# P in two pieces, pinned loads for the second mixture, and another hand-written opening

## The chip, the cores and the metric

The kernel runs on one core of one Trainium2 chip. The metric is the device time of one execution in microseconds, here the median of three runs of the kernel before: 829.34 us (828.67 to 830.78).

## The reference, cut to what matters

Four batches of an attention with eight heads go through two mixtures (two-layer networks). A short P (32 rows per head) first attends to K and V; its result is then both the keys and the values for Q.

```python
q, k, v: (4, 8, 576, 64)     p: (4, 8, 32, 64)
p_packed = sm_attn(p, k, v)              # softmax(p k^T / 8) v, 32 rows per head
out = sm_attn(q, p_packed, p_packed)     # 576 rows per head
x = out as (2304, 512)                   # tokens by (head, dim)
h = x @ w1_in;  x = (h * tanh(softplus(h))) @ w1_out     # 512 -> 2048 -> 512, Mish
h = x @ w2_in;  y = elu(h) @ w2_out                      # 512 -> 2048 -> 512, ELU
```

All four weights arrive as float64; the kernel reads them as pairs of 32-bit words and makes float32 numbers out of them itself.

## The kernel before, in words

**Weights.** A weight tile is 128 rows by 512 float64 numbers (512 KB). `load_raw` (L123) issues its load on SP's queue. `decode` (L135) gives the steps s0 to s5 that turn it into float32: s0 on ACT rescales one word in place (for the first eight tiles with the function Prelu, L158, otherwise with Copy, L160); s1 to s3 on DVE shift and join the words (L165, L173, L178); for w1o and w2 tiles s4 on ACT makes the upper part (L200) and s5 on DVE the rest (L206), since each product is made of three matmuls on upper and lower parts. Tiles of w1i go without s4 and s5: they are folded first (`fold`, L511: the product of the packed P with w1i, L519, which gives the weights G of this batch for the first layer; its two DVE subtractions and ACT copies are in `post`). Half of the tiles of the second mixture are decoded while the first mixture runs, split, and written back to HBM ("staged", L192). Their raw tiles have a pool of two buffers of their own (`sg`).

**Attention.** `scores1` multiplies K by P (L302), after DVE has turned both by 32x32 blocks (kT at L281, pT at L781). Its maximum is taken on DVE (L316), its exponentials on ACT (L321). `transpose_a1` turns the result on PE (L348), `packed` multiplies by V (L373) and turns the packed P (L403 to L406, PT). `scores2` multiplies Q by PT (`pe_rows`, L426), turns the scores on DVE (L455), and makes softmax on DVE and ACT (L462 to L471); `back` turns the result into the layer's input x as an upper and a lower part, a2h and a2l.

**Mixture 1** runs over 128 steps of one block of 288 tokens and 128 of the 2048 columns: `gemm1` (L550 to L552), `mish` on ACT and DVE (L559 to L561), and `gemm2` (L578 to L580) two steps later. The 32 tiles of w1 are decoded as they are needed; attention of the next batch and folds are put in between. In steps 34 to 93 `step_w2` decodes staged tiles of the second mixture. **Mixture 2** (L633 to L678) does the same with blocks of 512 tokens.

**What sets the order.** The first batch's attention, the decoding of the first eight tiles of w1 (indices 0 to 7: four of w1i, four of w1o) and the fold of the first 512 columns are written by hand: the list `order` in `startup` (L785) is the order on PE, DVE, ACT and SP there. `hk` and `hq` are the turns of K and Q, `sc`, `ta`, `pk` the steps of `scores1`, `transpose_a1` and `packed` for the two halves of the heads, `s2` those of `scores2`, `f0` those of the fold, `parts(n, i, ...)` the steps s_i of tile n. All other code is ordered by the compiler's scheduler, which may move an instruction ahead of those written before it when its inputs and its buffer are free; `keep_in_program_order` ties an instruction behind the one traced last on its engine. Each engine and each queue works strictly in order. In the opening, K, Q and weights are issued on SP's queue, V on ACT's, P on both (L756); a load also waits until the load eight places earlier has landed, because eight completion semaphores go round.

Of the kernel before, what the change touches and what calls it, by code (L numbers as in the profile page):

```python
# [9 lines left out]
F32 = mybir.dt.float32  # L10
F32R = mybir.dt.float32r
I32 = mybir.dt.int32
# [25 lines left out]
WSCALE = 2.0 ** 8  # L38
# [3 lines left out]
def kernel(  # L42
# [12 lines left out]
    nc = tc.nc  # L55
    B, H, S, D = q.shape
    NP = p.shape[2]
# [15 lines left out]
    dp = ctx.enter_context(tc.tile_pool(name="dp", bufs=3))  # L73
# [8 lines left out]
    def slot(shape, dt, name):  # L82
        return up.tile(shape, dt, tag="u", name=name)
# [27 lines left out]
        return spare.pop()[:, 1, :]  # L111

    ident = const.tile([128, 128], F32, name="ident")
    pT = const.tile([128, B * H // 2, 2, NP], F32, name="pT")

    y_dr = [dr.tile([128, 4, HALF], F32, name=f"y_dr{i}") for i in range(2 * B)]
    w2_dr = {}
# [5 lines left out]
    def load_raw(name, r, c):  # L123
        nm = f"raw_{name}{r}_{c}"
        t = slot([128, 1024], I32, nm) if name[1] == "1" else sg.tile([128, 1024], I32, tag="sg", name=nm)
        nc.sync.dma_start(
            out=t, in_=weights[name][r * 128:(r + 1) * 128, c * 1024:(c + 1) * 1024]
        )
        raws[name, r, c] = t

    w1v = {}
# [3 lines left out]
    def decode(name, r, c, staged=False, exps=False):  # L135
        raw = raws.pop((name, r, c))
        rr = raw.rearrange("p (n two) -> p n two", two=2)
        w0, w1 = rr[:, :, 0], rr[:, :, 1]
        t = dp.tile([128, 512], I32, tag="dec", name="dec")
        f1 = w1.bitcast(F32)  # L140
        whole = name == "w1i"
        key = {"w1i": (c, r // 2), "w2i": (name, c, r // 2)}.get(name, (name, r // 2))
        if staged:
            if r % 2 == 0:
                w2_dr[key] = dr.tile([128, 2, 2, 512], F32, name=f"w2_dr{name}{r}_{c}")
            parts = raw.bitcast(F32R).rearrange("p (x n) -> p x n", x=2)
        elif r % 2 == 0:
            if whole:
                w1v[key] = slot([128, 2, 512], F32, f"w1v{c}_{r}")
            else:  # L150
                wt[key] = [(small if name == "w2o" and r >= 12 else slot)([128, 2, 512], F32R, f"{name}{x}{r}_{c}") for x in "hl"]
        oi = w1v[key][:, r % 2, :].bitcast(I32) if whole else t

        def s0():
            tc.keep_in_program_order(
                nc.scalar.activation(out=f1, in_=f1, func=ACTF.Prelu, scale=REBIAS, alpha=2.0 ** 32)  # L158
                if exps
                else nc.scalar.activation(out=f1, in_=f1, func=ACTF.Copy, scale=REBIAS)  # L160
            )

        def s1():
            tc.keep_in_program_order(
                nc.vector.tensor_scalar(  # L165
                    out=t, in0=w1, scalar1=3, scalar2=0xFFFFFFF8 - 2 ** 32 if exps else 0x7FFFFFF8,
                    op0=ALU.logical_shift_left, op1=ALU.bitwise_and,
                )
            )

        def s2():
            if not exps:
                nc.vector.scalar_tensor_tensor(  # L173
                    out=t, in0=w1, scalar=-0x80000000, in1=t, op0=ALU.bitwise_and, op1=ALU.bitwise_or
                )

        def s3():
            nc.vector.scalar_tensor_tensor(  # L178
                out=oi, in0=w0, scalar=29, in1=t, op0=ALU.logical_shift_right, op1=ALU.bitwise_or
            )  # L180

        def s4():
            if whole:
                if r % 2 == 1:
                    nc.gpsimd.dma_start(out=w1_dr[c * 2 + r // 2], in_=w1v[key])
            else:
                split_hi(t.bitcast(F32), parts[:, 0] if staged else wt[key][0][:, r % 2, :], 1.0 / WSCALE)

        def s5():
            if staged:  # L190
                split_lo(t.bitcast(F32), parts[:, 0], parts[:, 1], 1.0 / WSCALE)
                nc.gpsimd.dma_start(out=w2_dr[key][:, r % 2], in_=parts.bitcast(F32))  # L192
            elif not whole:
                hi, lo = wt[key]
                split_lo(t.bitcast(F32), hi[:, r % 2, :], lo[:, r % 2, :], 1.0 / WSCALE)

        return [s0, s1, s2, s3, s4, s5]

    def split_hi(val, hi, factor=1.0):
        nc.scalar.activation(out=hi, in_=val, func=ACTF.Copy, scale=factor)  # L200
# [90 lines left out]
    def scores1(b, s):  # L291
        d = {}

        def pe():
            ps = pm()
            d["pair"] = last_pair[0]
            for x in range(2):
                for g in (3, 2, 1, 0):
                    kg = kT[b, g].rearrange("p e s -> p (e s)").rearrange("p (j x t) -> p j x t", x=2, t=32)
                    for th in range(2):  # L300
                        r = 64 * s + 32 * th
                        nc.tensor.matmul(  # L302
                            out=ps[th][32 * g:32 * g + 32, 0:HALF],
                            lhsT=pT[r:r + 32, b * 4 + g, x, :],
                            rhs=kg[r:r + 32, :, x, :],
                            start=(x == 0),
                            stop=(x == 1),
                        )
            if s:
                for g in range(4):  # L310
                    kT.pop((b, g))
# [199 lines left out]
    def fold(b, c):  # L511
# [17 lines left out]
            for s in range(2):  # L529
                split(d["ps"][s], G[b, c][0][:, s, :], G[b, c][1][:, s, :], 1.0 / WSCALE)  # L530

        return [pe, post]


    gt1, ht = {}, {}
# [212 lines left out]
    DEC1 = P["DEC1"]  # L748

    def startup():  # L750
        pr = slot([128, B * H // 2, D], F32, "pr")
        ps_ = p.rearrange("b (g s) n d -> s n (b g) d", s=2)
        for s in range(2):
            for th in range(2):
                r = 64 * s + 32 * th
                (nc.sync, nc.scalar)[s].dma_start(out=pr[r:r + 32], in_=ps_[s])  # L756
        make_identity(nc, ident)
        if WARM:
            wu = ps_h.tile([128, 512], F32, tag="h", name="warm")
# [18 lines left out]
        def parts(n, *which):  # L778
            return [dec[n][i] for i in which]

        nc.vector.transpose(  # L781
            out=pT.rearrange("p g x k -> p (g x k)"), in_=pr.rearrange("p g d -> p (g d)")
        )
        a1t0, a1t1 = ta
        order = [  # L785
            hk[0][0], hk[1][0], hk[2][0], hk[3][0], sc[0][0], sc[1][0], *parts(0, 0), *parts(0, 1, 3, 4, 5),
            sc[0][1], *parts(1, 0), sc[1][1], *parts(1, 1, 3, 4, 5), sc[0][2], a1t0[0], a1t0[1], pk[0][0], a1t1[0], a1t1[1],
            hq[0][0], hq[1][0], sc[1][2], *parts(2, 0), *parts(3, 0), pk[0][1], pk[1][0], hq[2][0], hq[3][0], pk[1][1], pk[0][2],
            *parts(2, 1, 3), pk[1][2], s2[0], *parts(2, 4, 5), *parts(3, 1, 3, 4, 5), f0[0], s2[1], s2[2],
            s2[3], s2[4], *parts(4, 0), f0[1], s2[5], *parts(4, 1, 3), s2[6], *parts(4, 4), s2[7], *parts(4, 5),  # L790
            *parts(5, 0, 1, 3, 4, 5), *parts(6, 0, 1, 3, 4, 5), *parts(7, 0, 1, 3, 4, 5),
        ]
        for o in order:
            o()
# [153 lines left out]
```

## Time and profile before

| | us |
|---|---|
| median of three runs | 829.34 |
| lowest, highest | 828.67, 830.78 |
| the profiled execution's own time | 830.86 |
| its span in the trace | 829.1 |
| PE busy in the span | 777.5 (94%) |
| DVE busy | 440.1 (53%) |
| ACT busy | 346.6 (42%) |

The span lies 1.76 us below the time of the execution that it belongs to. Busy shares over the whole span hide the stages: what counts is read from stretches of it. "Idle before" in a row is the time in which the engine stood still ahead of it, and behind the arrow stands what ended that. PEclk is the clock granted to TensorE as a share of 2.4 GHz.

### The profile page before, as it was taken

How to read it: one execution, taken by the hardware profiler on the slowest of the kernel's cores; microseconds unless marked ns; L12 is line 12 of the kernel's file. 1: busy time of each engine (PE TensorE's matmuls, PEld its weight loads, DVE VectorE, ACT ScalarE, POOL GpSimd, SP SyncE). 2: the span in 40 equal slices, each digit the busy share in tenths (PEclk: the TensorE clock that was granted, in tenths of full speed). 3: DMA queues.
4: the chain of work that ended last, by engine and by line, in shares of the span. 5: the costliest groups of instructions: out<-in, count | busy, mean ns of one | idle time of the engine just before them, and what ended most of it. 6: DMA issues, size and time to landing. Idle time of an engine off the chain costs nothing.

```text
span 829.1 us, 13056 instructions
## 1 busy us (share of the span) xinstructions
PE 777.5 (94%) x5212; PEld 671.0 (81%) x5212; DVE 440.1 (53%) x844; ACT 346.6 (42%) x676; POOL 22.6 (3%) x46
## 2 busy tenths in 40 slices
PE   3656898999999999999999999999999999999997
PEld 3344788979989898899998888888888888888886
DVE  3678788675587466772516753513253334342342
ACT  1265774557465655674534432312141223221222
POOL 0000000000101000000000000000000000000000
PEclk7565998999999999999999999999999999999999
DMA  9954377237656656431592310200020001000000
GB/s 273 372 215 158 120 272 220 81 111 222 197 198 244 191 142 233 142 116 51 180 332 79 127 52 26 76 1 1 1 76 14 1 0 51 13 0 1 26 26 26
DMA packets 69181, 96.80 MB, mean 117 GB/s; under 512 B 36096, under 2 KB 44800, under 8 KB 69120
## 3 DMA queue, kind: packets, MB, share of 16 engines
q1 hardware_dynamic: 62176, 77.22, 29.6%
q0 software_dynamic: 4736, 17.30, 5.3%
q10 hardware_dynamic: 2208, 1.44, 0.7%
q8 instruction: 41, 0.67, 0.3%
q14 instruction: 20, 0.16, 0.1%
HBM read 73.92 MB, written 22.02 MB: 116 GB/s over the span
## 4 chain that ended last, share of the span: by engine, by line
PE 85%; DVE 6%; ACT 4%; DMA 3%; issue 1%; SPq 0%; ACTq 0%; DVEq 0%
PE h L640 8%; PE h L641 8%; PE h L642 8%; PE o L663 8%; PE o L664 8%; PE o L665 8%; PE acc L579 7%; PE acc L578 7%; PE acc L580 7%; PE h L550 4%; PE h L551 4%; PE h L552 4%; PE pm L519 1%; DMA raw_w1i<-in_moe_w_in_dram 1%; DMA raw_w2i<-in_moe_w_in_dram 1%
## 5 line engine op out<-in xcount | busy, mean ns | idle before, releaser
L578 PE MATMUL acc<-gh,w1oh 128*128 128x288 f32 x512 | 150.1, 300 | 5.6 <-ACT w1oh L200 3.4
L579 PE MATMUL acc<-gl,w1oh 128*128 128x288 f32 x512 | 152.8, 300 | 0.1
L580 PE MATMUL acc<-gh,w1ol 128*128 128x288 f32 x512 | 152.3, 300 | 0.0
L641 PE MATMUL h<-yl,w2ih 128*128 128x512 f32 (+1 forms) x320 | 117.7, 368 | 0.0
L642 PE MATMUL h<-yh,w2il 128*128 128x512 f32 (+1 forms) x320 | 117.5, 368 | 0.0
L640 PE MATMUL h<-yh,w2ih 128*128 128x512 f32 (+1 forms) x320 | 116.7, 368 | 0.0
L663 PE MATMUL o<-w2oh,gh 128*128 128x512 f32 x288 | 112.4, 390 | 1.1 <-ACT ob L269 0.7
L664 PE MATMUL o<-w2ol,gh 128*128 128x512 f32 x288 | 112.2, 390 | 0.0
L644 ACT ACTIVATE t<-h 128x512 f32<-128x512 f32 (+1 forms) x80 | 42.8, 553 | 165.3 <-PE h L642 157.5
L665 PE MATMUL o<-w2oh,gl 128*128 128x512 f32 x288 | 108.3, 389 | 0.0
L645 DVE TENSOR_SCALAR t<-t 128x512 f32<-128x512 f32 (+1 forms) x80 | 31.7, 399 | 142.3 <-ACT t L644 141.5
L578 PEld LDWEIGHTS acc<-gh,w1oh 128*128 128x128 f32 x512 | 96.9, 192 | 10.1 <-ACT w1oh L200 3.8
L579 PEld LDWEIGHTS acc<-gl,w1oh 128*128 128x128 f32 x512 | 97.7, 191 | 6.5 <-DVE gl L561 3.2
L580 PEld LDWEIGHTS acc<-gh,w1ol 128*128 128x128 f32 x512 | 97.5, 191 | 5.0 <-issue 4.5
L561 DVE TENSOR_TENSOR gl<-t,gh 128x288 fp32r<-128x288 f32 x128 | 57.8, 453 | 77.9 <-ACT gh L560 77.3
L550 PE MATMUL h<-a2h,gh 128*128 128x288 f32 x256 | 78.7, 310 | 14.4 <-ACT a2h L200 10.5
L559 ACT ACTIVATE t<-h 128x288 f32<-128x288 f32 x128 | 52.2, 409 | 81.4 <-PE h L552 80.1
L551 PE MATMUL h<-a2l,gh 128*128 128x288 f32 x256 | 77.8, 304 | 2.9 <-DVE a2l L204 2.9
L200 ACT ACTIVATE gh<-t 128x512 fp32r<-128x512 f32 (+1 forms) x80 | 46.6, 588 | 78.6 <-DVE t L646 49.5
L552 PE MATMUL h<-a2h,gl 128*128 128x288 f32 x256 | 77.1, 303 | 0.0
L204 DVE TENSOR_TENSOR gl<-t,gh 128x512 fp32r<-128x512 f32 (+1 forms) x80 | 50.3, 638 | 41.0 <-ACT gh L200 39.5
L642 PEld LDWEIGHTS h<-yh,w2il 128*128 128x128 f32 x320 | 60.3, 188 | 10.3
(107 smaller groups left out, 1101.5 us busy)
## 6 DMA issues: line engine op xcount, KB each, us to landing
w1r<-w_dr SPq DMA_DIRECT2D x24, 512.0 KB, 6.4
raw_w2i<-in_moe_w_in_dram SPq DMA_DIRECT2D x16, 512.0 KB, 4.4
raw_w1i<-in_moe_w_in_dram SPq DMA_DIRECT2D x16, 512.0 KB, 8.1
raw_w1o<-in_moe_w_out_dram SPq DMA_DIRECT2D x16, 512.0 KB, 8.1
raw_w2o<-in_moe_w_out_dram SPq DMA_DIRECT2D x16, 512.0 KB, 3.7
k<-in_k_dram SPq DMA_DIRECT2D x16, 288.0 KB, 4.6
y_dr<-y POOLq DMA_DIRECT2D x16, 288.0 KB, 2.9
w_dr<-w1v POOLq DMA_DIRECT2D x8, 512.0 KB, 5.1
```

The lines of the kernel that those rows point to most:

```text
L550: nc.tensor.matmul(out=hp, lhsT=wh, rhs=xh, start=(kt == 0), stop=False)
L551: nc.tensor.matmul(out=hp, lhsT=wh, rhs=xl, start=False, stop=False)
L552: nc.tensor.matmul(out=hp, lhsT=wl, rhs=xh, start=False, stop=(kt == 1))
L578: nc.tensor.matmul(out=o, lhsT=wh[:, cs], rhs=gh, start=first, stop=False)
L579: nc.tensor.matmul(out=o, lhsT=wh[:, cs], rhs=gl, start=False, stop=False)
L580: nc.tensor.matmul(out=o, lhsT=wl[:, cs], rhs=gh, start=False, stop=last)
L640: nc.tensor.matmul(out=hp, lhsT=wh, rhs=xh, start=(i == 0), stop=False)
L641: nc.tensor.matmul(out=hp, lhsT=wh, rhs=xl, start=False, stop=False)
L642: nc.tensor.matmul(out=hp, lhsT=wl, rhs=xh, start=False, stop=(i == 3))
L663: nc.tensor.matmul(out=o, lhsT=gh[:, ts], rhs=wh, start=(kk == 0), stop=False)
L664: nc.tensor.matmul(out=o, lhsT=gh[:, ts], rhs=wl, start=False, stop=False)
L665: nc.tensor.matmul(out=o, lhsT=gl[:, ts], rhs=wh, start=False, stop=(kk == NK - 1))
```

## The change

P is loaded as two tiles, one for batch 0 (a quarter of it, on SP's and ACT's queues) and one for batches 1 to 3 (four loads on POOL's queue, placed after the first instruction of the identity matrix and ahead of the others). The first is turned where the whole was turned; the second at the end of the hand-written list. Loads of raw tiles of w2 are tied to program order on SP's queue. Tiles of w1i are decoded in place in their result. The fold of batch 0's first 512 columns has its upper and lower parts in two steps. The list `order` is another one.

```diff
-    pT = const.tile([128, B * H // 2, 2, NP], F32, name="pT")
+    pT = [const.tile([128, n * H // 2, 2, NP], F32, name=f"pT{n}") for n in (1, B - 1)]
...
-        nc.sync.dma_start(
+        ins = nc.sync.dma_start(
             out=t, in_=weights[name][r * 128:(r + 1) * 128, c * 1024:(c + 1) * 1024]
         )
+        if name[1] == "2":
+            tc.keep_in_program_order(ins)
...
-        oi = w1v[key][:, r % 2, :].bitcast(I32) if whole else t
+        wv = w1v.get(key)
+        oi = wv[:, r % 2, :].bitcast(I32) if whole else dp.tile([128, 512], I32, tag="dec", name="dec")
+        t = oi
...
+        def post_hi():
+            G[b, c] = [slot([128, 2, 512], F32R, f"g{x}{b}_{c}") for x in "hl"]
+            for s in range(2):
+                split_hi(d["ps"][s], G[b, c][0][:, s, :], 1.0 / WSCALE)
+
+        def post_lo():
+            for s in range(2):
+                split_lo(d["ps"][s], G[b, c][0][:, s, :], G[b, c][1][:, s, :], 1.0 / WSCALE)
+
+        return [pe, post] if b or c else [pe, post_hi, post_lo]
...
-        pr = slot([128, B * H // 2, D], F32, "pr")
+        pr = [slot([128, n * H // 2, D], F32, f"pr{n}") for n in (1, B - 1)]
         ps_ = p.rearrange("b (g s) n d -> s n (b g) d", s=2)
-        for s in range(2):
-            for th in range(2):
-                r = 64 * s + 32 * th
-                (nc.sync, nc.scalar)[s].dma_start(out=pr[r:r + 32], in_=ps_[s])
+        for x, (a, n) in enumerate(((0, H // 2), (H // 2, (B - 1) * H // 2))):
+            for s in range(2):
+                for th in range(2):
+                    r = 64 * s + 32 * th
+                    eng = nc.gpsimd if x else (nc.sync, nc.scalar)[s]
+                    eng.dma_start(out=pr[x][r:r + 32], in_=ps_[s][:, a:a + n, :])
...
-            hk[0][0], hk[1][0], hk[2][0], hk[3][0], sc[0][0], sc[1][0], *parts(0, 0), *parts(0, 1, 3, 4, 5),
+            hk[0][0], hk[1][0], hk[2][0], hk[3][0], sc[0][0], sc[1][0], sc[0][1], sc[1][1], *parts(0, 0), sc[0][2],
```

On SP's queue at the start of the program, before (`k_*`, `q_*` are Q and K of batch 0 by pairs of heads; `raw_w2i` a tile of the second mixture, `raw_w1i` of the first):

```order
L756 DMA pr<-in_p_dram 32x16x64 x2
L249 DMA k_0_142<-in_k_dram 128x576
L249 DMA k_1_144<-in_k_dram 128x576
L249 DMA k_2_146<-in_k_dram 128x576
L249 DMA k_3_148<-in_k_dram 128x576
L126 DMA raw_w2i_1_1924<-in_moe_w_in_dram 128x1024
L126 DMA raw_w2i_1_1926<-in_moe_w_in_dram 128x1024
L126 DMA raw_w1i_0_163<-in_moe_w_in_dram 128x1024
L126 DMA raw_w1i_0_165<-in_moe_w_in_dram 128x1024
L249 DMA q_0_167<-in_q_dram 128x576
```

And now:

```order
L771 DMA pr_117<-in_p_dram 32x4x64 x2
L253 DMA k_0_148<-in_k_dram 128x576
L253 DMA k_1_150<-in_k_dram 128x576
L253 DMA k_2_152<-in_k_dram 128x576
L253 DMA k_3_154<-in_k_dram 128x576
L127 DMA raw_w1i_0_169<-in_moe_w_in_dram 128x1024
L127 DMA raw_w1i_0_171<-in_moe_w_in_dram 128x1024
L253 DMA q_0_173<-in_q_dram 128x576
```

The two loads of `raw_w2i` now stand behind the loads of K for batch 2, and the first two of `raw_w2i_3` behind the reloads of the staged tiles at the start of mixture 2.

On DVE at the start of the program, before (`sm` holds the maximum of the first scores, `dec` and `w1v` a tile of w1i under way):

```order
L281 STREAM_TRANSPOSE kT_3_212<-k_3_148 128x576
L165 TENSOR_SCALAR dec<-raw_w1i_0_163 128x512
L178 SCALAR_TENSOR_TENSOR w1v_0_192<-raw_w1i_0_163,dec 128x512
L316 TENSOR_REDUCE sm<-pm 128x1
L317 TENSOR_SCALAR sm<-sm 128x1
```

And now:

```order
L285 STREAM_TRANSPOSE kT_3_214<-k_3_154 128x576
L320 TENSOR_REDUCE sm<-pm 128x1
L321 TENSOR_SCALAR sm<-sm 128x1
L320 TENSOR_REDUCE sm<-pm 128x1
L321 TENSOR_SCALAR sm<-sm 128x1
L337 TENSOR_SCALAR rs<-sm 128x1
L340 RECIPROCAL rs<-rs 128x1
L275 COPY a1t_0_272<-pm 128x512
L275 COPY a1t_0_272<-pm 64x128
L285 STREAM_TRANSPOSE qT_0_306<-q_0_173 128x576
```

The decode of the first tile of w1i moved from ahead of the maximum to behind the first turns of Q.

On ACT at the end of the hand-written list, before (`t` is Mish, `raw_w1o` the step s0 of a tile of w1o, `w1oh` its upper part):

```order
L559 ACT_TABLE_LOAD
L559 ACTIVATE t_488<-h_481 128x288
L560 ACTIVATE gh_489<-t_488 128x288
L559 ACTIVATE t_513<-h_506 128x288
L560 ACTIVATE gh_514<-t_513 128x288
L559 ACTIVATE t_534<-h_527 128x288
L200 ACTIVATE w1oh_0_198<-dec 128x512
L158 ACT_TABLE_LOAD
L158 ACTIVATE raw_w1o_0_183<-raw_w1o_0_183 128x512
L560 ACTIVATE gh_535<-t_534 128x288
L559 ACT_TABLE_LOAD
L559 ACTIVATE t_585<-h_578 128x288
```

And now:

```order
L162 ACTIVATE raw_w1o_0_185<-raw_w1o_0_185 128x512
L162 ACTIVATE raw_w1o_0_187<-raw_w1o_0_187 128x512
L204 ACTIVATE a2h_431<-a2t_0_433 128x576
L162 ACTIVATE raw_w1o_0_189<-raw_w1o_0_189 128x512
L162 ACTIVATE raw_w1o_0_191<-raw_w1o_0_191 128x512
L204 ACTIVATE a2h_431<-a2t_1_445 128x576
L572 ACT_TABLE_LOAD
L572 ACTIVATE t_489<-h_482 128x288
L204 ACTIVATE w1oh_0_199<-dec 128x512
L573 ACTIVATE gh_490<-t_489 128x288
L572 ACTIVATE t_513<-h_506 128x288
L573 ACTIVATE gh_514<-t_513 128x288
```

All four s0 with Prelu now stand ahead of the first Mish; in the whole program ACT has four table loads fewer.

## Rows read from the trace of the kernel before

**Rows 1.** Windows: busy us (instructions) by engine, clock, DMA share, GB/s.
```profile
10.00:20.00 10.00, 1.19 (x48) 0.50 (x30) 1.98 (x5) 1.93 (x2) 0.00 (x0) 0.57 1.06 285
23.90:34.50 10.60, 9.91 (x168) 5.25 (x176) 6.55 (x15) 1.87 (x4) 0.54 (x1) 0.50 1.01 402
34.50:51.00 16.50, 3.11 (x21) 1.45 (x22) 13.49 (x25) 5.18 (x9) 0.00 (x0) 0.60 0.97 365
51.00:71.90 20.90, 12.73 (x69) 11.24 (x67) 16.34 (x31) 14.43 (x23) 0.53 (x1) 0.74 0.20 59
71.90:127.00 55.10, 47.47 (x445) 39.19 (x445) 46.09 (x95) 38.22 (x78) 2.89 (x5) 0.90 0.63 212
140.00:400.00 260.00, 259.43 (x2281) 235.65 (x2280) 165.54 (x332) 151.13 (x315) 16.15 (x30) 1.00 0.50 159
```

**Rows 2.** Timeline, beginning: start, us, engine, line, what, idle before and releaser.
```profile
1.36 5.39 PE L761 MATMUL warm<-ident 128*128 128x128 f32 x32 [1.36 <-POOL ident masks.py:199]
5.30 1.25 DVE L781 STREAM_TRANSPOSE pT<-pr 128x1024 f32<-128x1024 f32 x1 [5.30 <-DMA pr<-in_p_dram]
9.24 1.95 PE L302 MATMUL pm<-kT,pT 32*32 32x288 f32 x64 [2.49 <-DVE kT L281]
17.27 0.65 ACT L158 ACTIVATE raw_w1i<-raw_w1i 128x512 f32<-128x512 f32 x1 [2.43 <-DMA raw_w1i<-in_moe_w_in_dram]
19.02 0.75 DVE L316 TENSOR_REDUCE sm<-pm 128x1 f32<-128x576 f32 x1
23.91 1.42 DVE L281 STREAM_TRANSPOSE qT<-q 128x576 f32<-128x576 f32 x2
31.39 0.43 DVE L271 COPY pt<-pm 64x256 f32<-64x256 f32 x1
34.53 1.58 DVE L455 STREAM_TRANSPOSE x<-pm 128x288 f32<-128x288 f32 x4 [1.53 <-PE pm L426]
```

**Rows 3.** Timeline of SP's queue, beginning: start, us until issued, line, what.
```profile
3.67 1.27 SPq L126 DMA_DIRECT2D raw_w2i<-in_moe_w_in_dram  x2
10.66 2.81 SPq L126 DMA_DIRECT2D raw_w1i<-in_moe_w_in_dram  x2
13.72 2.24 SPq L249 DMA_DIRECT2D q<-in_q_dram  x4
```

**Rows 4.** Waits of SP's queue, 0 to 110 us: total, times, longest.
```profile
SPq L126 <- DMA raw_w2i<-in_moe_w_in_dram: 5.7, 1, 5.7
```

**Rows 5.** DMA issues, first 20 us: count, KB each, median us to landing.
```profile
q<-in_q_dram SPq DMA_DIRECT2D x4, 288.0 KB, 7.3
v<-in_v_dram ACTq DMA_DIRECT2D x4, 160.0 KB, 7.6
```

**Rows 6.** Groups by line, POOL, shapes apart: busy us, mean ns.
```profile
L185 POOL DMA_DIRECT2D w_dr<-w1v x8 | 4.6, 580 | 119.3 <-DVE w1v L178 92.9 <-DVE rs L333 21.9 <-DVE pv L386 4.5
```

**Rows 7.** Timeline of DVE, ACT and PE, 40 to 72 us, as rows 2.
```profile
45.99 0.69 DVE L178 SCALAR_TENSOR_TENSOR dec<-raw_w1o,dec 128x512 int32<-128x512 int32 x1
55.84 1.28 ACT L158 ACT_TABLE_LOAD   x1
57.14 0.67 ACT L158 ACTIVATE raw_w1o<-raw_w1o 128x512 f32<-128x512 f32 x1
60.87 1.28 ACT L158 ACT_TABLE_LOAD   x1
62.86 0.43 DVE L165 TENSOR_SCALAR dec<-raw_w1o 128x512 int32<-128x512 int32 x1 [1.28 <-DMA raw_w1i<-in_moe_w_in_dram]
71.96 1.96 PE L519 MATMUL pm<-w1v,pt 64*32 64x512 f32 x16 [4.73 <-DVE w1v L178]
```

**Rows 8.** Tile raw_w2i: ns min/median/max, first and last start; landing; SP's queue.
```profile
L160 ACT ACTIVATE raw_w2i<-raw_w2i x16: 656/666/688, 174.9 to 455.2; 128x512 f32<-128x512 f32 x16
DMA to landing us min/median/max: 2.9/4.3/8.3
156.34 9.73 SPq L249 DMA_DIRECT2D k<-in_k_dram  x4
```

More of the change, by code (lines that the diff above doesn't have):

```diff
@@ L138, in decode @@
         w0, w1 = rr[:, :, 0], rr[:, :, 1]
-        t = dp.tile([128, 512], I32, tag="dec", name="dec")
         f1 = w1.bitcast(F32)
@@ L184, in s4 @@
                 if r % 2 == 1:
-                    nc.gpsimd.dma_start(out=w1_dr[c * 2 + r // 2], in_=w1v[key])
+                    nc.gpsimd.dma_start(out=w1_dr[c * 2 + r // 2], in_=wv)
             else:
@@ L303, in pe @@
                             out=ps[th][32 * g:32 * g + 32, 0:HALF],
-                            lhsT=pT[r:r + 32, b * 4 + g, x, :],
+                            lhsT=pT[b > 0][r:r + 32, max(b - 1, 0) * 4 + g, x, :],
                             rhs=kg[r:r + 32, :, x, :],
@@ L530, in post @@
                 split(d["ps"][s], G[b, c][0][:, s, :], G[b, c][1][:, s, :], 1.0 / WSCALE)
-        return [pe, post]
+        def post_hi():
[6 more added lines that the diff above has]
+        return [pe, post] if b or c else [pe, post_hi, post_lo]
     gt1, ht = {}, {}
@@ L779, in parts, with turn_p @@
             return [dec[n][i] for i in which]
-        nc.vector.transpose(
-            out=pT.rearrange("p g x k -> p (g x k)"), in_=pr.rearrange("p g d -> p (g d)")
-        )
+        def turn_p(x):
+            nc.vector.transpose(
+                out=pT[x].rearrange("p g x k -> p (g x k)"), in_=pr[x].rearrange("p g d -> p (g d)")
+            )
+        turn_p(0)
         a1t0, a1t1 = ta
         order = [
-            hk[0][0], hk[1][0], hk[2][0], hk[3][0], sc[0][0], sc[1][0], *parts(0, 0), *parts(0, 1, 3, 4, 5),
[L787 to L791, printed above, removed]
+            hk[0][0], hk[1][0], hk[2][0], hk[3][0], sc[0][0], sc[1][0], sc[0][1], sc[1][1], *parts(0, 0), sc[0][2],
+            a1t0[0], a1t0[1], a1t1[0], a1t1[1], *parts(1, 0), pk[0][0], hq[0][0], hq[1][0], sc[1][2], *parts(0, 1, 3, 4),
+            pk[1][0], pk[0][1], hq[2][0], hq[3][0], pk[0][2], pk[1][1], *parts(2, 0), *parts(3, 0), *parts(1, 1, 3, 4),
+            pk[1][2], s2[0], *parts(2, 1, 3, 4), *parts(3, 1, 3, 4), s2[1], s2[2], f0[0], s2[3], s2[4], f0[1],
+            *parts(4, 0), *parts(5, 0), s2[5], f0[2], *parts(6, 0), *parts(7, 0), s2[6], s2[7],
+            *parts(4, 1, 3, 4), *parts(5, 1, 3, 4), *parts(4, 5), *parts(6, 1, 3, 4), *parts(5, 5), *parts(7, 1, 3, 4),
+            *parts(6, 5), *parts(7, 5), lambda: turn_p(1),
         ]
```

## Prediction

> **What bounds the kernel now.** I read the busy time by stretches first [rows 1]. From 140 to 400 us PE is busy 259.43 of 260 us, and it stays so to the end: what is saved there must be PE work, and the change takes none away. Before that PE is not the bound. In the stretch 71.9 to 127 it is busy 47.47 of 55.1 us while DVE is busy 46.09, with the decoding of w1; in 51 to 71.9 DVE is busy 16.34 of 20.9; in 34.5 to 51 it is 13.49 of 16.5; in 23.9 to 34.5 only 6.55 of 10.6; in 10 to 20 no engine does anything for more than 2 us while the DMA engines are full (share 1.06). So the beginning is a chain through loads, then DVE, and every microsecond by which the chain ends earlier shifts all that follows. The one number to follow is when DVE has made the second part of w1i, for which PE waits at 71.96 (4.73 us idle) [rows 7].
>
> Then the timeline of the beginning [rows 2, 3]. The scores of K are finished at 9.24 + 1.95 = 11.19, but DVE takes their maximum at 19.02, since in its order the decode of the first tile of w1i stands ahead; that waits for ACT's step at 17.27, and that for the load. The load was issued at 10.66, behind two loads of raw_w2i of 512 KB each, which nobody needs before 174.9 [rows 8]; SP stood 5.7 us for one of them to land [rows 4]. Q is issued behind, at 13.72, and takes 7.3 us to land [rows 5], so about 21 to 23.
>
> Last, ACT from 55.84 to 62.15 [rows 7]: three table loads of 1.28 us, the first and the last of which are shown, around two steps s0 of w1o, since these are Prelu and stand between Mish. DVE's decode at 62.86 follows right behind the second of them; the row names a load as releaser, but the instruction decodes the tile that ACT had just finished. That is why DVE has 4.56 us of idle time in this stretch.
>
> **The change part by part.**
>
> *Loads, and the maximum ahead of the decode.* Gone from the queue ahead of w1i and Q: 2 x 512 KB of w2i. P's first piece is a quarter. K is issued as before (raw_w2i came next on SP, at 3.67 [rows 3]); the first w1i load then waits only for the last K to land. I put that near 8 us (DVE turned the last K before 9.24), so it is issued 2.7 us earlier than at 10.66. Q's loads wait for loads of V issued from about 4 us on; with 7.6 us to landing [rows 5] they are issued at about 11, and with 7.3 us land at about 18; as 1 MB less is in flight (3.6 us at the 285 GB/s of rows 1), I take 17.5 for the first. Bounds: 15.5 (all of the 1 MB gained and the first issue at 10) and 21 (nothing gained, as before). The maximum no longer waits for w1i: from 11.2 on, two maxima, four exponentials, the turn on PE and the copy took from 19.02 to 23.91 with a decode of 1.1 in between, so DVE is ready for Q at 15 to 16. So Q's landing sets the start of its turns: 17.5 against 23.91.
>
> From there to the last copy of PT, DVE has two pairs of turns (2 x 1.42), two decodes (2 x 1.12: 0.43 and 0.69, [rows 7]), two copies (2 x 0.43) and about 1 us of small steps (an estimate): 7.0, against 7.9 before with PE's waits in it. Last copy at 24.5 instead of 31.82. `pe_rows` then needs what it needed before until its scores are turned: 34.53 - 31.82 = 2.7. The turn at L455 starts at **27.2 instead of 34.53: -7.3**. Two decodes of w1i (2.2) lie in these 2.7 as before.
>
> *34.5 to 51.* DVE is busy 13.49 of 16.5. The decode of a w1o tile (1.1) leaves this stretch, and the fold's subtractions move behind the first half of the softmax, so that they no longer wait for ACT. 13.5 - 1.1 = 12.4; I add 0.5 for rest waits: 12.9. **-3.6** (bounds: -1.1 if the 3.0 us of idle time stay, -4.1).
>
> *51 to 71.9.* DVE's 16.34 grow by the decode that came over (1.1), the turn of P for batches 1 to 3 (768 of 1024 columns of 1.25 us: 0.9 [rows 2]), and by two steps of the next w1o tile that now stand ahead of the last w1i (1.1): 19.5. The three table loads go from ACT (3.85 us), and the four s0 stand in ACT's free time before. Of the 4.56 us of idle time I keep 1.5, an estimate between none and all. 21.0 against 20.9: **+0.1** (bounds -1.4, +3.2).
>
> The Trainium skill ("ScalarE: Activation LUTs", What ACT_TABLE_LOAD costs) puts a switch at 1.28 us plus a drain of 1.38. Here the row at 55.84 ends at 57.12, and ACT's next instruction starts at 57.14: the load's length agrees, the drain is not there. By the page the three loads would be worth 8.0 instead of 3.85 us, and the sum 4.1 better.
>
> *71.9 to 127.* The 1.1 us done ahead are missing here: **-1.1**, as DVE is the bound. A fourth table load goes from ACT just behind 71.96; hidden, nothing.
>
> *P's second piece* must be there when it is turned, some 25 us later than the first: hidden. Its four issues on POOL stand ahead of the identity, and PE's 16 warming products wait for that at 1.36. An issue takes 0.58 on POOL for 128 rows [rows 6]; for 384 rows of P I bound it by 0.58 and by 3 x 0.58 = 1.7: identity 2.3 to 7 us later, the products (5.39 us long) end at 9.1 to 13.7 instead of 6.75, K's scores start between 9.2 and 13.7. I take the lower: DVE then waits for Q anyway. At the upper end the turns of Q start at 16 + 4.5 = 20.5, that is +3.0.
>
> The Trainium skill ("DMA: Bandwidth & Descriptors", Anatomy of one DMA) says that many descriptors can be emitted before the cost of one more shows. By it the lower bound holds; no row here has an issue of so many short rows.
>
> *Pinned loads.* raw_w2i is now issued behind the loads of K for batch 2, which end at 156.34 + 9.73 = 166.1, and lands 4.3 us later (2.9 to 8.3) at 170.9, against its use at 174.9 [rows 8]; all of these shift together. Cover of 4 us, cost nothing; if it went, ACT would stand for the load, and PE, which follows ACT two steps behind, soon after. Decoding w1i in place and the split fold add and remove no instruction.
>
> Sum: -7.3 - 3.6 + 0.1 - 1.1 = -11.9. Against the profiled execution's 830.86 (1.5 above the median) that is 819.0; against the median 817.4. As each stretch was packed without a new wait except the 2 us named, and 71.9 to 127 has waits of its own that need not shift whole, I take 1.6 us off: a gain of 10.3, **819.0 us** as the median to come.
>
> **The rivals.**
>
> *The loads don't come earlier.* DMA is full from 10 to 50 us; V and Q might land as late as before, so that the first term shrinks to the 1.0 us of packing and the better order remains: -1.0 - 3.6 + 0.1 - 1.1 = -5.6, about 824. For: share 1.06 in 10 to 20. Against: 1.05 MB less are to be moved before Q.
>
> *The identity is late.* POOL's four issues at the upper bound: +3.0 on the forecast, 822.
>
> *The middle takes it back.* In 71.9 to 127 PE waits and DVE's idle 9 us may come from loads and buffers rather than from DVE; if half of the gain is lost there, about 824. For: PE is at 47.47 of 55.1. Against: DMA share only 0.63.
>
> *Slower: a pinned load holds ACT.* ACT works in order; if SP's queue is held by a K load so that raw_w2i lands more than 4 us late, ACT stands in the stretch where PE is never idle, and so again with raw_w2i_3 behind the reloads at mixture 2's start. PE's lead of two steps set aside, it costs the delay less the 4 us of cover; it decides from a delay of 14.3 us (4 and the gain of 10.3), and at 20 us the time is 819 + 16 = 835. For: nothing is ahead of need by more than these 4 us. Against: the K loads wait for buffers by 9.73 us in all, and shift with the rest.
>
> **How the numbers follow.** Forecast 0.66, loads 0.12, identity 0.07, middle 0.10, slower 0.05. The forecast's own range: with Q at 15.5 and no rest waits -2.0 - 2.0 - 1.0 gives 814; with 3 us of idle time kept in the two stretches 822. Including the loads and the middle to 826 the range is 813.5 to 826; beyond lie the slower case and about half a tenth on either side. A measurement of this kernel can tell 0.3% (2.5 us) from no change: faster 0.91 (a tenth of the loads and middle cases ends within it), same 0.04, slower 0.05.
>
> **What would show it.** The maximum of the first scores at 11 to 14 us instead of 19.02; Q's first turn at 16 to 19; the turn of the second scores near 27; no table load between the first Mish and the second fold; the second fold's product at 60 to 62 instead of 71.96, and from there the same distances to the end. Wrong, if the second fold stands near 61 and the end near 825 or above (the middle), if the turn of Q stays above 21 (the loads), if the warming products end beyond 12 (the identity), or if ACT stands for raw_w2i.

## The result and the profile after

| | before | after |
|---|---|---|
| median, us | 829.82 (4 runs) | 819.32 (4 runs) |
| lowest, highest | 828.67, 830.78 | 818.59, 822.30 |
| profiled execution, its span | 830.86, 829.1 | 819.25, 817.5 |

The ratio is 0.9881, with a 95% interval of 0.9853 to 0.9909: 10.5 us faster by the medians, 11.6 by the spans. 819.0 was forecast.

The timeline of the changed kernel's beginning, all engines, columns as in [rows 2]; it answers to [rows 2, 3, 6 and 7]:

```profile
1.37 2.59 POOL L771 DMA_DIRECT2D pr<-in_p_dram  x4 [0.43 <-issue]
4.40 6.23 PE L776 MATMUL warm<-ident 128*128 128x128 f32 x32 [4.40 <-POOL ident masks.py:199]
11.64 0.78 DVE L285 STREAM_TRANSPOSE kT<-k 128x576 f32<-128x576 f32 x1 [2.17 <-DMA k<-in_k_dram]
11.64 0.80 SPq L127 DMA_DIRECT2D raw_w1i<-in_moe_w_in_dram  x2
12.55 2.23 SPq L253 DMA_DIRECT2D q<-in_q_dram  x4
14.41 0.76 DVE L320 TENSOR_REDUCE sm<-pm 128x1 f32<-128x576 f32 x1 [1.99 <-PE pm L306]
19.34 1.53 DVE L285 STREAM_TRANSPOSE qT<-q 128x576 f32<-128x576 f32 x2 [0.51 <-DMA q<-in_q_dram]
28.07 1.58 DVE L459 STREAM_TRANSPOSE x<-pm 128x288 f32<-128x288 f32 x4
39.17 1.58 DVE L208 TENSOR_TENSOR a2l<-a2t,a2h 128x576 fp32r<-128x576 f32 x2
39.98 1.28 ACT L572 ACT_TABLE_LOAD   x1
51.08 0.97 DVE L797 STREAM_TRANSPOSE pT<-pr 128x768 f32<-128x768 f32 x1
59.26 1.96 PE L523 MATMUL pm<-w1v,pt 64*32 64x512 f32 x16 [6.11 <-DVE w1v L182]
```

The maximum comes 4.6 us earlier than before, the turn of Q 4.6, the turn of the second scores 6.5, the second fold 12.7. The load of w1i, however, is issued at 11.64, later than the 10.66 of before: what SP waits for is the last K, which now lands just ahead of 11.64 and was turned before 9.24 in the kernel before. The warming products end at 10.63, 3.9 us later than before; PE's next row starts at 12.48, after a wait of 1.84 us for the last turn of K. No table load stands between 39.98 and the second fold.

Windows of the changed kernel at the same stages, columns as in [rows 1]: the wait for loads, the second scores up to x's last part, from there to the second fold, and PE's full stretch:

```profile
10.00:20.00 10.00, 7.04 (x112) 4.50 (x110) 4.52 (x10) 4.86 (x13) 0.00 (x0) 0.66 1.07 300
28.07:40.75 12.68, 3.58 (x21) 1.57 (x22) 12.23 (x23) 6.66 (x11) 0.56 (x1) 0.63 1.03 411
40.75:59.26 18.51, 10.96 (x70) 10.05 (x68) 18.48 (x37) 8.64 (x18) 0.53 (x1) 0.87 0.67 243
140.00:400.00 260.00, 259.45 (x2282) 235.67 (x2281) 166.59 (x333) 151.80 (x315) 15.07 (x28) 1.00 0.52 165
```

In the second and third row DVE is busy 30.71 of 31.19 us, where it was busy 29.83 of 37.4 before [rows 1]: the change has taken its idle time away, not its work. The last row is that of before: PE is full, and nothing was to be had there.

| stretch, from - to | before | forecast of the change | after | measured |
|---|---|---|---|---|
| start - turn of second scores | 34.53 | -7.3 | 28.07 | -6.5 |
| - end of a2l | 16.43 | -3.6 | 12.68 | -3.8 |
| - second fold | 21.0 | +0.1 | 18.51 | -2.5 |
| - end of the span | 757.14 | -1.1 | 758.24 | +1.1 |

### The profile page after: what moved, and what is told of

Its sections match the earlier page's. It is cut to its first block, busy times and chain, and to the rows that moved or that the text cites. A ratio compares the mean times of both kernels' runs of the same rounds, so it can differ in the third digit from the quotient of the medians.

```text
span 817.5 us, 13068 instructions
## 1 busy us (share of the span) xinstructions
PE 776.2 (95%) x5212; PEld 669.6 (82%) x5212; DVE 439.6 (54%) x845; ACT 341.2 (42%) x672; POOL 25.0 (3%) x50
## 4 chain that ended last, share of the span: by engine, by line
PE 85%; DVE 7%; DMA 4%; ACT 3%; issue 1%; ACTq 0%; SPq 0%; DVEq 0%
PE h L654 8%; PE h L655 8%; PE h L653 8%; PE o L676 8%; PE o L677 8%; PE o L678 8%; PE acc L592 7%; PE acc L591 7%; PE acc L593 7%; PE h L563 4%; PE h L564 4%; PE h L565 4%; PE pm L523 1%; DMA raw_w1o<-in_moe_w_out_dram 1%; DMA v<-in_v_dram 1%
## 5 line engine op out<-in xcount | busy, mean ns | idle before, releaser
L653 PEld LDWEIGHTS h<-yh,w2ih 128*128 128x128 f32 x320 | 60.3, 188 | 10.3
```

Of the source, the lines that this page charges most:

```text
L653: nc.tensor.matmul(out=hp, lhsT=wh, rhs=xh, start=(i == 0), stop=False)
```

## The experiments

All twelve were timed in five rounds against the kernel before, which had a median of 829.96 to 830.33 in these jobs. "End" is the span less the start of the second fold, both of the profiled execution; w1i is its first issue, and K and Q stand for the last turn of K and the first of Q; a dash stands where a trace has all turns of K in one row, which then ended by 10.0. The beginning of e9 is that of the changed kernel, and that of e10 and e11 is e6's: the second folds of these three lie 1.4 us apart (58.67, 57.31 and 57.67), so one profile does not tell a smaller difference there.

| kernel | median | ratio, 95% | w1i | K | Q | second fold | end |
|---|---|---|---|---|---|---|---|
| e1: ties left out | 823.13 | 0.9899-0.9928 | 13.00 | 11.07 | 21.67 | 62.62 | 757.4 |
| e2: P whole | 818.54 | 0.9838-0.9876 | 8.76 | - | 17.50 | 56.59 | 759.5 |
| e3: old list | 826.67 | 0.9943-0.9973 | 10.95 | 10.96 | 22.32 | 69.86 | 753.5 |
| e4: before + ties | 828.83 | 0.9969-0.9987 | 8.75 | - | 21.92 | 70.37 | 757.8 |
| e5: before, s0 ahead | 826.48 | 0.9941-0.9966 | 10.41 | - | 23.75 | 68.18 | 757.1 |
| e6: P's rest on SP | 813.74 | 0.9787-0.9813 | 9.34 | 9.35 | 18.06 | 58.67 | 753.7 |
| e7: P whole + POOL loads | 820.30 | 0.9872-0.9903 | 12.49 | 12.49 | 20.49 | 60.38 | 760.6 |
| e8: Q first | 822.69 | 0.9897-0.9930 | 12.21 | - | 12.66 | 61.21 | 761.9 |
| e9: after + products | 819.83 | 0.9865-0.9898 | 11.47 | 11.48 | 18.58 | 59.04 | 758.1 |
| e10: e6 + 15 products | 816.99 | 0.9833-0.9862 | 9.43 | 9.44 | 17.08 | 57.31 | 757.9 |
| e11: e6 + 10 products | 813.16 | 0.9782-0.9811 | 9.66 | 9.67 | 17.31 | 57.67 | 752.8 |
| e12: P's rest behind V | 816.26 | 0.9827-0.9867 | 9.49 | 9.14 | 20.65 | 60.25 | 753.6 |

**The parts one by one (e1 to e5).** e1 takes the ties of `raw_w2i` out of the changed kernel, e2 loads and turns P whole, e3 puts the old list into the changed kernel; e4 puts the ties alone into the kernel before:

```diff
-        if name[1] == "2":
-            tc.keep_in_program_order(ins)
```

> The changed kernel without the tie of the second mixture's loads: the two loads of raw_w2i (1.05 MB) stand ahead of w1i and Q again. Theory A (the loads carry the first part of the gain): Q lands some 4 us later (1.05 MB at 250 GB/s), its first turn starts near 23 instead of 19.3, time about 823. Theory B (the new order carries nearly all, since w1i and Q were issued in the changed kernel at 11.6 and 12.6 us, hardly earlier than before): Q's turn within 1 us of 19.3, time 819 to 820.

> The changed kernel with P in one piece, loaded and turned as before. Theory A: 0.39 MB more ahead of K on the two queues, the turn of P 0.9 us longer in the opening: scores later, 820.5 to 821.5. Rival (V, issued earlier after the small first piece, and POOL's queue took the rate from K in the changed kernel, whose last turn of K started at 11.6 instead of 8.4): K's last turn back near 8.5, scores near 9.3, but Q still gates: time 818.5 to 819.5.

> The changed kernel (ties, P in two pieces, decode in place) with the old hand-written order. Theory A: the first part of the gain stays: the turn of the second scores near 29 to 30, time 824 to 825. Theory B: the decode of w1i again holds the maximum until its load has landed near 18, the table loads are back: second fold near 70, time 828 to 830.

> The kernel before with the tie of the second mixture's loads alone. Theory A: w1i is issued near 8 instead of 10.7, lands near 14 instead of 17.2, all 3 us earlier: 826.5. Theory B: the freed rate goes to V and K, 828.5 to 830.

By time, e1 came out as its Theory A said, e2 as its rival and e4 as its Theory B; e3 lies between its two theories, with the second fold of B (69.86). The list is worth the most: between e3 and the changed kernel 7.3 us by the medians, 6.4 by the ratios, and at the second fold even 10.6 (69.86 to 59.26); 4.7 of these are lost again behind it, where e3's end is the shorter. The ties are worth 3.8 by the medians, 2.7 by the ratios, with the new list (e1), and about 1.5 with the old one (e4; by its interval 1.1 to 2.6). With the old list w1i is issued at 8.75, but the maximum still stands behind its decode and comes at 17.02, 2 us earlier than before. P in pieces gains nothing: e2's time lies within the uncertainty of the changed kernel's, and its second fold 2.7 us ahead. The timeline of e2, with P whole:

```profile
8.76 1.04 SPq L127 DMA_DIRECT2D raw_w1i<-in_moe_w_in_dram  x2
10.68 2.02 SPq L253 DMA_DIRECT2D q<-in_q_dram  x4
17.50 1.44 DVE L285 STREAM_TRANSPOSE qT<-q 128x576 f32<-128x576 f32 x2 [2.17 <-DMA q<-in_q_dram]
26.13 1.58 DVE L459 STREAM_TRANSPOSE x<-pm 128x288 f32<-128x288 f32 x4
```

These stand beside the forecast's 8, 11, 17.5 and 27.2, which the changed kernel missed: without its split of P all are within 1.1 us, the last one earlier than forecast.

e5 moves three instructions in the list of the kernel before, so that four table loads go from ACT; nothing else in the kernel's text changes:

```diff
-            s2[3], s2[4], *parts(4, 0), f0[1], s2[5], *parts(4, 1, 3), s2[6], *parts(4, 4), s2[7], *parts(4, 5),
-            *parts(5, 0, 1, 3, 4, 5), *parts(6, 0, 1, 3, 4, 5), *parts(7, 0, 1, 3, 4, 5),
+            s2[3], s2[4], *parts(4, 0), f0[1], *parts(5, 0), *parts(6, 0), *parts(7, 0), s2[5], *parts(4, 1, 3), s2[6], *parts(4, 4), s2[7], *parts(4, 5),
+            *parts(5, 1, 3, 4, 5), *parts(6, 1, 3, 4, 5), *parts(7, 1, 3, 4, 5),
```

> The kernel before, with one edit: in the hand-written list the three later steps s0 of w1o (tiles 5, 6 and 7, Prelu) stand right behind the fold's subtractions and ahead of the first Mish, so that ACT has four table loads fewer (21 instead of 25). Loads, P and everything else are as before. Theory A (the table loads delay DVE's decode): three loads of 1.28 us go between 54 and 62, DVE keeps more of its idle time for work, the second fold's product starts 2.5 to 4 us before 71.96, and the time is 826 to 828. Theory B (DVE's chain is full and the loads lay beside it; or ACT, which works in order, is held by the raw w1o tiles that it now asks for earlier): second fold within 1 us of 71.96, time 829 to 831.

Theory A holds. The second fold comes 3.78 us earlier and the time falls by 3.5. Of the 3.78 us 0.16 were gained ahead of the stretch (the second scores are turned at 34.37 instead of 34.53), so that the three table loads, 3.84 us long, were worth 3.6. The window of e5 from 51 us to just ahead of its second fold at 68.18: DVE is idle 1.19 us, where it was idle 4.56 in 51.00 to 71.90 [rows 1].

```profile
51.00:68.00 17.00, 11.57 (x68) 10.58 (x66) 15.81 (x31) 8.52 (x17) 0.53 (x1) 0.80 0.23 73
```

**Why K is late (e6, e7).** In the changed kernel two things differ from e2 at the start: V is issued at 2.61 instead of 4.00, and POOL's queue carries four loads of 96 KB. e6 keeps the early V and puts the four loads on SP behind those of w1; e7 keeps P whole and adds four such loads on POOL into a tile that nobody reads:

```diff
-                    eng = nc.gpsimd if x else (nc.sync, nc.scalar)[s]
+                    eng = nc.sync if x else (nc.sync, nc.scalar)[s]     # e6, traced behind load_w1(6)
...
+        again = slot([128, (B - 1) * H // 2, D], F32, "again")          # e7, on P whole
+                nc.gpsimd.dma_start(out=again[r:r + 32], in_=ps_[s][:, H // 2:, :])
```

> The changed kernel, with P's second piece issued on SP's queue behind the loads of w1 instead of on POOL's queue; V is still issued early (about 2.6), since ACT's queue has only a quarter of P ahead of it. In the changed kernel the last K is turned at 11.64 and Q at 19.34; with P whole the last K is turned at 9.54 and Q at 17.50. Theory P (the four loads on POOL, many short rows, slow K's landing and hold the identity): last K turned at 8.5 to 9.7, w1i issued at 8 to 9, Q turned at 17 to 18, second fold near 57 and time 816 to 818. Theory V (V issued 1.3 us earlier shares the DMA engines with K): last K still turned at 11 to 12, Q at 19, second fold near 59, time 819.

> The changed kernel with P loaded and turned whole, and beside it four more loads of the last three quarters of P on POOL's queue, ahead of the identity, into a tile that nobody reads (work added; V is issued at about 4.0 again, as with P whole). Theory P (these loads slow K's landing): last K turned near 11, w1i issued near 11, Q turned near 19, second fold near 58.5, time 819 to 821. Theory V: as with P whole, last K at 9.5, Q at 17.5, second fold at 56.6, only the warming products end later (near 10.6 instead of 7), time 818 to 819.

Theory P holds in both for K: without POOL's loads the last K is turned at 9.35, with them at 11.64 and 12.49. Behind K each missed a part of it: e6's time is 2.3 us below its range, with a second fold 1.7 later than forecast, and e7's second fold is 1.9 later than forecast. The DMA issues of the first 20 us (count, KB each, median us to landing) and all that was moved in them, in e2:

```profile
DMA packets 4870, 5.74 MB, mean 287 GB/s; under 512 B 2413, under 2 KB 3437, under 8 KB 4870
k<-in_k_dram SPq DMA_DIRECT2D x4, 288.0 KB, 4.7
v<-in_v_dram ACTq DMA_DIRECT2D x4, 160.0 KB, 5.4
```

and in e7:

```profile
DMA packets 4554, 4.83 MB, mean 241 GB/s; under 512 B 2417, under 2 KB 3441, under 8 KB 4554
k<-in_k_dram SPq DMA_DIRECT2D x4, 288.0 KB, 6.7
v<-in_v_dram ACTq DMA_DIRECT2D x4, 160.0 KB, 8.1
again<-in_p_dram POOLq DMA_DIRECT2D x4, 96.0 KB, 7.1
```

0.39 MB more to move, and K lands 2.0 us later, V 2.7; the rate falls from 287 to 241 GB/s. The last K is 2.95 us later, the second fold 3.8. By the medians e7 loses 1.8; its profiled execution is at the upper end of its runs. The bytes alone would take 1.4 us at 287 GB/s. The Trainium skill ("DMA: Bandwidth & Descriptors", Queues, rings and completion order) says that each DMA engine goes round the queues that have work, a packet at a time; that a third queue takes its share while K and V are under way agrees with these rows. Why the rate falls as well, no run here shows. It need not be the third queue: e12 below has none and issues the same four loads on ACT's queue, and in its first 20 us 5.08 MB were moved.

e6 gained 5.6 us on the changed kernel by the medians, more than forecast, though in the profile its second fold is only 0.6 earlier, less than such readings scatter. The rest lies behind it: its end is 4.5 shorter. The waits of PE from 58 to 127 us (total, times, longest), in the changed kernel:

```profile
PE acc L591 <- DVE y L275: 2.6, 2, 2.1
PE h L563 <- ACT t L572: 2.5, 2, 1.5
PE pm L523 <- ACT e L325: 1.2, 1, 1.2
```

and in e6, where the second and third are gone:

```profile
PE pm L409 <- DVE pv L390: 1.0, 1, 1.0
PE acc L591 <- DVE y L275: 0.7, 1, 0.7
```

The code behind the list is the same text in both; the compiler's scheduler orders it, and ordered it otherwise once the beginning was otherwise (in the traces some 30 of DVE's 845 instructions stand elsewhere). In the changed kernel the maximum of the second batch's scores waits on DVE behind decodes, and the switch of tables for its exponentials follows. DVE and ACT of the changed kernel:

```profile
70.11 0.75 DVE L320 TENSOR_REDUCE sm<-pm 128x1 f32<-128x576 f32 x1
73.04 1.28 ACT L325 ACT_TABLE_LOAD   x1
74.33 0.53 ACT L325 ACTIVATE e<-pm,sm 128x320 f32<-128x320 f32 x1
```

and of e6:

```profile
67.72 0.75 DVE L320 TENSOR_REDUCE sm<-pm 128x1 f32<-128x576 f32 x1
70.66 1.28 ACT L325 ACT_TABLE_LOAD   x1
```

Over the same stretch, though, the granted clock of TensorE is half (1.2 GHz) up to 66 us in e6 and up to 70.8 in the changed kernel. Windows 68 to 70 us of the changed kernel and of e6; the column before the last two is the granted clock:

```profile
68.00:70.00 2.00, 2.00 (x10) 2.00 (x9) 2.00 (x5) 0.43 (x2) 0.00 (x0) 0.50 0.00 0
```
```profile
68.00:70.00 2.00, 2.00 (x18) 2.00 (x17) 2.00 (x4) 0.72 (x2) 0.00 (x0) 1.00 0.00 0
```

PE is busy throughout in both and gets through 10 instructions in one and 18 in the other. Order or clock had to be told apart.

**Order or clock (e9, e10, e11).** Products of the identity with itself fill PE's wait ahead of the second fold:

```diff
             ps = d["ps"] = pm()
+            if (b, c) == (0, 1):
+                for i in range(15):                                       # e11: 10
+                    tc.keep_in_program_order(nc.tensor.matmul(out=ps[0][:, 0:128], lhsT=ident, rhs=ident))
```

> The changed kernel with 15 products of the identity with itself on PE, tied among the products just before the second fold (work added, which nobody reads); the order on DVE, ACT and SP is that of the changed kernel. There PE stands 6.1 us before the second fold at 59.26, the granted clock falls from 1.00 to 0.50 near 57 and comes back at 70.8, while PE is busy most of the time. Theory C (the clock is what costs behind the second fold): PE is busy up to the fold, the clock stays near 1.00 up to 70, PE's 10 us of busy time between 59 and 71 take about half, and the time is 815 to 816.5, 3 to 4 below 819.3. Theory D (DVE bounds this stretch, idle only 2.5 us between 59 and 71, so PE's clock hardly matters): the clock stays high but the time falls by no more than 1.5, 818 to 819.5. Slower, if the added products push those of the first steps behind the fold: 820 to 822.

> The kernel with P's second piece on SP's queue (813.74) and the same 15 added products ahead of the second fold. The scheduler then orders the middle on DVE, ACT and SP as in the changed kernel, not as in the run of 813.74, so that this kernel differs from the one before in this list by its opening alone: the second fold near 58.7 instead of 59.26. Theory O (the 4.6 us that the run of 813.74 gained behind the second fold come from the order of the middle): this kernel is slower than 813.74, near the one with the added products in the changed kernel less 0.6 (814.5 to 818.5). Theory C (they come from the clock, which came back at 66.2 instead of 70.8): 811 to 814, as the clock now stays high.

> The kernel with P's second piece on SP's queue and 10 added products ahead of the second fold; here the scheduler leaves the order on DVE, ACT and SP as in the run of 813.74 to the row. Opening and second fold as there (58.7). Theory C: the clock stays at 1.00 over the second fold where it was 0.50 from 56 to 66, and the time is 810 to 812.5. Theory D or O: the clock is higher but DVE bounds the stretch, 813 to 814.5.

The windows 58 to 72 us. The changed kernel and e9:

```profile
58.00:72.00 14.00, 12.00 (x83) 8.58 (x84) 11.32 (x21) 6.87 (x14) 1.06 (x2) 0.54 0.49 165
```
```profile
58.00:72.00 14.00, 12.26 (x90) 9.31 (x91) 11.97 (x23) 7.67 (x16) 1.07 (x2) 0.63 0.49 164
```

e10 and e11:

```profile
58.00:72.00 14.00, 12.84 (x107) 9.89 (x92) 11.73 (x22) 8.93 (x17) 0.09 (x1) 0.77 0.42 143
```
```profile
58.00:72.00 14.00, 13.06 (x112) 10.28 (x96) 10.35 (x20) 9.44 (x21) 0.44 (x1) 0.80 0.44 148
```

The products do not keep the clock at full speed, as Theories C and D of e9 took for granted: in e9 it still falls to half near 60 us, though PE's wait ahead of the fold is 2.9 us instead of 6.1. In 58 to 72 us it is higher by a sixth, and the time is no less (819.83, 0.3 beyond what Theory D allowed). That alone is a weak test of the clock, since most of the stretch is still at half.

More is seen over the whole middle. By their traces e9 and e10 have DVE's and ACT's instructions in the order of the changed kernel (e10 but for one exchange on each), and e11 has them in that of e6. The windows 59 to 127 us of the changed kernel and e10:

```profile
59.00:127.00 68.00, 58.60 (x512) 48.75 (x513) 55.16 (x112) 42.27 (x88) 2.66 (x5) 0.84 0.64 205
```
```profile
59.00:127.00 68.00, 56.41 (x522) 49.02 (x517) 55.53 (x114) 43.27 (x90) 2.13 (x4) 0.91 0.64 207
```

and of e6 and e11:

```profile
59.00:127.00 68.00, 63.42 (x553) 53.27 (x538) 57.21 (x118) 44.26 (x94) 2.72 (x5) 0.87 0.68 212
```
```profile
59.00:127.00 68.00, 62.34 (x559) 54.13 (x552) 58.19 (x118) 44.64 (x95) 2.37 (x4) 0.92 0.69 216
```

With the first order the clock is 0.84 and 0.91, and the ends are 758.2 and 757.9; with the other it is 0.87 and 0.92, and they are 753.7 and 752.8. A clock higher by 0.05 to 0.07 goes with an end that is 0.3 to 0.9 us shorter, the other order with one that is 4.5 to 5.1 shorter. What a full clock would bring, no run shows.

e10 and e11 alone, timed side by side, share their opening; their second folds stand 0.36 apart and their clocks are alike. Theory O holds: 816.99 against 813.16, with intervals apart. The waits of PE from 58 to 127 us in e10:

```profile
PE acc L594 <- DVE y L275: 4.2, 2, 3.3
PE h L566 <- ACT t L575: 3.4, 2, 2.4
```

and in e11, where that for `t` is gone:

```profile
PE acc L594 <- DVE y L275: 1.4, 2, 1.0
```

The order of the middle is worth 3.8 us by the medians. Which of its moves does it was not tried.

**Two other beginnings (e8, e12).** e8, on e2, issues Q ahead of V and w1i and turns it in the wait for the first softmax; e12, on e6, issues P's rest on ACT's queue behind V and turns it ahead of Q:

```diff
+            hq[0][0], hq[1][0], hq[2][0], hq[3][0], sc[0][2], a1t0[0], ...          # e8
...
+            load_vt(0, kt, nc.scalar)
+        load_p(1)                                                                   # e12, nc.scalar
+            ... pk[0][0], lambda: turn_p(1), hq[0][0], hq[1][0], ...
```

> The changed kernel with P loaded and turned whole; Q's loads are issued ahead of V and of the first tiles of w1i, Q's turns stand in DVE's wait for the first softmax, and the decode of w1i comes later in the list. Theory A (Q's landing sets the start of the second scores): Q turned near 13 to 15 instead of 17.50, the turn of the second scores 1.5 to 3 us before 26.13, second fold at 54 to 55 instead of 56.59, time 816 to 817. Theory B (V and w1i now land last and hold the packing, and what was saved on Q is waited for there; DVE's work up to the second fold is the same): second fold 56 to 58, time 818 to 820.

> The kernel with P's second piece on SP's queue (813.74), but that piece issued on ACT's queue behind V and turned on DVE right ahead of the first turn of Q, where DVE stands 2.15 us for Q's landing at 18.06, instead of at the end of the hand-written list, where DVE has no idle time. The scheduler's order of the middle is near that of the run of 813.74 (the maximum of the second batch's scores stands at the same place). Theory A (the turn of 0.97 us goes into idle time, the four issues on ACT do not hold the exponentials): Q turned at 18 to 18.3, second fold at 57.4 to 57.9 instead of 58.67, time 812 to 813.3. Theory B (the issues on ACT behind V, some 1.6 us, hold the first exponentials, or the 384 KB land in Q's way): Q turned at 19 or later, second fold at 58.7 or later, time 814 to 816.

Both missed, as their rivals said, and by more than these: e8's 822.69 lies above its rival's 818 to 820, e12's 816.26 just above 814 to 816. In e8 Q is turned at 12.66, but V is issued at 6.18 over 7.40 us, and ACT is free for the exponentials only at 13.61: their result reaches DVE at 17.40, where e2 had it at 14.44. Then the packing still waits on PE for V, whose loads stand behind Q's:

```profile
20.53 3.07 PE L377 MATMUL pm<-v,a1t 128*32 128x64 f32 x80 [2.10 <-DMA v<-in_v_dram]
```

In e12 the four issues hold ACT for 3.28 us, where 1.6 was taken, and the exponentials wait for them. ACT of e12, and the row of P's issues there (ns min/median/max):

```profile
9.81 3.28 ACTq L772 DMA_DIRECT2D pr<-in_p_dram  x4
13.12 1.28 ACT L785 ACT_TABLE_LOAD   x1 [13.12 <-DMA v<-in_v_dram]
14.42 0.53 ACT L325 ACTIVATE e<-pm,sm 128x320 f32<-128x320 f32 x1
L772 ACTq DMA_DIRECT2D pr<-in_p_dram x6: 317/441/631, 0.7 to 12.8; - x6
```

One issue takes 0.63 us at most, so at least 0.8 of the 3.28 is waiting, as a load waits for the one eight places earlier. That is also what holds Q, whose loads stand behind P's in this count and are issued over 6.18 us from 11.07 on. SP's waits up to 22 us in e12:

```profile
SPq L253 <- DMA pr<-in_p_dram: 4.3, 1, 4.3
```

The exponentials' result reaches DVE at 16.91, but DVE goes on only at 19.75, after 1.96 us of waiting for loads: the loads and not the exponentials ended last.

e6 and e11 are the fastest of all, 813.74 and 813.16, and the difference between the two is within their uncertainty.

## Why the prediction was right, and where it was not

**The opening, -7.3 forecast, -6.5 measured.** The mechanism held: the maximum left the wait for w1i, and Q's landing set the start of its turns, if only by a last wait of 0.51 us. The forecast's own signs were missed narrowly: the maximum at 14.41 (11 to 14), Q's first turn at 19.34 (16 to 19), the second fold at 59.26 (60 to 62); none of its signs of being wrong came. Two steps of it failed, and a shorter way behind them made up for a part. "K is issued as before", and so the first w1i load "near 8": it went at 11.64, since POOL's loads hold K's landing up (e6, e7). I had weighed POOL's loads for the time of their issue alone and not for what they take from K. The issues took 0.65 us each in the row at 1.37, near the lower bound of 0.58, so the identity was late by 3 us only, which nobody waited for. The Trainium skill's rule that many descriptors can be emitted before the cost of one more shows ("DMA: Bandwidth & Descriptors", Anatomy of one DMA) agrees with these 0.65 us for 384 rows. And Q's loads left at 12.55 over 2.23 us, where 11 was forecast, and the first Q was turned at 19.34, not 17.5. From there to the turn of the second scores it took 8.7 us, a microsecond less than I had counted. One reading in that count was wrong: in the kernel before only one decode of w1i lay in the 2.7 us between the last copy of PT and the turn (its other one stood ahead of the copy). Now two lie there, and the distance is 2.3, so the sum took no harm. The rival "the loads don't come earlier" is half of what happened, by another cause than its own: w1i was indeed no earlier.

**34.5 to 51, -3.6 and -3.8.** As worked out: DVE is busy 12.23 us, against 12.4 forecast, and its idle time is 0.45.

**51 to 71.9, +0.1 and -2.5.** The term that was most off. I kept 1.5 us of idle time on DVE; it has 0.03. I also counted 19.5 us of work by adding up durations, and DVE did 18.48: where nothing waits, rows overlap (one starts at 57.23 and takes 0.68 us, the next starts at 57.83). e5 shows what the table loads alone were worth here: 3.6 us of their 3.84. The row at 73.04 ends at 74.32 and the exponential starts at 74.33. The drain of 1.38 us of the Trainium skill ("ScalarE: Activation LUTs", What ACT_TABLE_LOAD costs) is again not there, and by e5 each load was worth 1.2 us and no more.

**71.9 to the end, -1.1 and +1.1.** Here the forecast had the sign wrong. I took the stretch as bound by DVE's work, so that work done ahead would be missing here. But its length hangs on an order that I had not looked at: the scheduler's. Over the changed kernel and the runs built on it the end runs from 752.8 to 761.9, and e10 and e11 show 3.8 us of it by order alone. Not all of that range is order: e8 has e2's order behind the opening, but a mean clock of 0.82 from the second fold to 140 us, where e2 has 0.88, and it ends 2.4 later. And that the 2.2 us between forecast and measurement are order was not shown for the kernel before and after themselves. The rival "the middle takes it back" had the place right, and as cause loads and buffers; what was seen is order.

**The sum.** -11.9 in parts stands against -11.6 in the spans, because the third term's error (-2.6) and the last's (+2.2) are of opposite sign: that the sum came out so near is luck. So is a part of the median's agreement. The 1.6 us that I took off for waits are not found in the spans, where the gain is 11.6; by the medians it is 10.5, since the profiled execution of before lay 1.0 above its median (830.86 against 829.82) and that of the changed kernel at it.

**P's second piece, "hidden".** Its landing was; its cost was not. Its turn of 0.97 us went from the beginning, where DVE waits for K, to where DVE has no idle time, and its loads delayed K. No run splits the 2.7 us by which e2's second fold is ahead between the two.

**The slower rival.** `raw_w2i` is issued at 154.56, and ACT takes the first at 163.3, without a wait for it; its loads land 4.2 us after their issue in the median. The cover was 8.7 us less that landing, and nothing used it up. The other pinned loads, `raw_w2i_3` behind the reloads, start at 417.97; from 140 us on PE's longest wait is 0.7 us, as in the kernel before.

## What to carry to other kernels

A load that nobody needs soon is not free just because its queue is idle: ask which transfers are under way at that moment and who waits for them. Where an engine has idle time in an early stage and none in a later one, a step should not be moved from the first to the second, however small. And where a scheduler orders what follows a hand-written part, compare its order before and after each edit: a change of 4 us there can be larger than what the edit was made for.

## What was not expected of the hardware

With four loads of 96 KB on a third DMA queue (e7 against e2, 0.39 MB) the 16 engines moved 4.83 instead of 5.74 MB in the first 20 us, with a DMA share of 0.97 in both; what of it is due to the queue is open. A DMA issue of P took 0.32 to 0.63 us on ACT's queue (e12) and 0.65 on POOL's. The six executions of e8 had a mean granted clock from 0.968 down to 0.957 and took from 821.08 up to 824.93 us. And the granted clock of TensorE fell to half near 60 us in e9, after PE had been busy 6.18 of the 8 us ahead of 58 and had stood idle 2.9 us ahead of the fold:

```profile
50.00:58.00 8.00, 6.18 (x49) 5.94 (x48) 8.00 (x17) 2.98 (x6) 0.00 (x0) 1.00 0.58 184
60.00:62.00 2.00, 1.30 (x11) 0.84 (x4) 1.38 (x2) 0.99 (x3) 0.00 (x0) 0.50 0.96 303
```
